# One hardware ring in planned order, the second channel matmul as seven products, and an earlier third batch: a change to a cosFormer-plus-mixer kernel

## The chip, the cores and the metric

The kernel runs on one core of a Trainium2 chip. The time is the device time of one execution in microseconds (us); lower is better. The profile comes from one execution; its span runs from the first to the last instruction.

## What is computed

Eight batches go through linear attention with cosine weights and then through a mixer layer, first over tokens, then over channels. From the reference, cut to what matters:

```python
B, H, S, D = q.shape                      # 8, 8, 576, 64
theta = np.pi / 2.0 * pos / S
def phi(x, c, s):
    r = np.maximum(x, 0.0)
    return np.concatenate([r * c, r * s], axis=-1)
q_p, k_p = phi(q, cos, sin), phi(k, cos, sin)
kv = np.einsum('bhsf,bhsd->bhfd', k_p, v)
z = np.sum(k_p, axis=2)
x = np.einsum('bhsf,bhfd->bhsd', q_p, kv) / (np.einsum('bhsf,bhf->bhs', q_p, z)[..., None] + 1e-06)
# x to (batch, 576, 512)
u = x + (np.maximum(x.T @ w_tok1, 0.0) @ w_tok2).T      # w_tok1 576x256, w_tok2 256x576
out = u + np.maximum(u @ w_ch1, 0.0) @ w_ch2            # w_ch1 512x1536, w_ch2 1536x512
```

## The kernel before, in words

A batch has 576 tokens. Two partitions share nine tokens: the even partition has the first four and the odd one the last four as token tiles 0 to 3, and the ninth is half of a fifth tile (j = 4, the tail). The tails of two batches are put together, so that channel work is done in nine groups of 4 x 128 tokens: groups 0 to 7 are the batches without their tails, group 8 holds all the tails (`group`, L277).

The attention of a batch runs over the five tiles j. `load` (L110) brings k, q and v as float32 into two sets of buffers (`raw`, b % 2), two DMAs each. `kfeat` and `qfeat` (L129, L134) make relu(x cos) and relu(x sin) of each tile in bfloat16: the cos half on VectorE (DVE, line L127), the sin half on ScalarE (ACT, L125). `vcast` (L145) casts v on GpSimd (POOL). `kv` (L165) multiplies features by v, with a column of ones for the sum z, in 40 matmuls of 65 columns; `kv_out` copies the result to SBUF on ACT. `qturn_dma` (L148) transposes a tile of q features by a DMA from SyncE's (SP's) queue. `num` (L186) multiplies them by kv, 8 matmuls a tile, and `x_out` (L194) adds 1e-6 to the denominator, inverts and multiplies on DVE.

The token mixer is `b1` (L206, 10 matmuls of 512 columns), `b1_out` (relu, ACT), `u_mm` (L224, two times four matmuls), `u_out` (L233, DVE: x is added, u is float32), `u_cast` (L237, ACT, to bfloat16) and `uturn_dma` (L244, two DMA transposes). For odd batches `tail_mm` and `tail_out` (L259, L270) do the tails of two batches.

The channel mixer of a group is `mlp1` (L282): 12 slots of four matmuls of 512 columns, each evicted with relu into `h1T` by `mlp1_out` (two of three on ACT, one on DVE); and `mlp2` (L296): four token tiles of 12 matmuls of 512 columns, in three parts each. `mlp2_out` (L301) adds u on DVE into a separate tile `res`, and ACT's queue stores it.

The order of work on each engine is written by hand. The head (up to about 24 us) does batch 0 in two halves of four heads. Then comes a stage with group 0's channel work, batch 1's attention and the loading and casting of the channel weights (L606 to L667). From there each group g has 24 slots, 12 of mlp1 and 12 parts of mlp2, and `plan_of(g)` (L718) puts the attention of later batches behind them: num, b1 and u of batch g + 1, and features, transposes and kv of batch g + 2. Group 1 is dense: it also has the features and kv of batch 2, and the plan loads batches 3 and 4 in it.

Transfers go over three queues: SP issues the first loads, the weights and all DMA transposes; ACT issues two weight loads and the stores; POOL issues the loads of batches 2 to 7. `load_late` (L709) lets POOL wait for a given eviction by a one-column copy before it issues loads.

Of the kernel before, what the change touches and what calls it, by code (L numbers as in the profile page):

```python
# [14 lines left out]
DEP = mybir.DependencyInfo(mybir.DependencyClass.Sync, mybir.DependencyReason.DATA)  # L15
# [3 lines left out]
def kernel(  # L19
# [14 lines left out]
    F = 2 * D  # L34
# [11 lines left out]

    NJ = 5  # L50
    T = 4

    const = ctx.enter_context(tc.tile_pool(name="const", bufs=1))

# [3 lines left out]

    ident = sb("ident", [P, P], BF16)
    cos_t = sb("cos_t", [P, NJ], F32)  # L60
    sin_t = sb("sin_t", [P, NJ], F32)
# [4 lines left out]
    wc2 = sb("w_ch2", [P, NCH, Dm], BF16)  # L66

    raw = {n: [sb(f"{n}_raw{i}", [P, H, NJ, D], F32) for i in range(2)] for n in "qkv"}
    kp = [sb(f"kp{j}", [P, H, 2, D], BF16) for j in range(NJ)]
    qp = [sb(f"qp{j}", [P, H, 2, D], BF16) for j in range(NJ)]  # L70
# [15 lines left out]
    res_all = sb("res", [P, 2, 2, Dm], F32)  # L86
    res = [res_all[:, i] for i in range(2)]
# [12 lines left out]


    def slots(b):

        return (0, 4) if b % 2 == 0 else (1, 0)

    def place(b, j):
        first, tail = slots(b)
        return tail if j == T else first + j

    def load(b, src, name, engs, h0=0, h1=None):  # L110
        h1 = H if h1 is None else h1
        dst = raw[name][b % 2]
        s = src[b].rearrange("h (i n) d -> i h n d", n=9)
        if b % 2 == 0:
            parts = ((1, 5, 9, 0), (0, 0, 5, 0))
        else:
            parts = ((0, 0, 4, 1), (1, 4, 9, 0))
        for (par, lo, hi, at), eng in zip(parts, engs):
            eng.dma_start(out=dst[par:P:2, h0:h1, at:at + hi - lo, :], in_=s[:, h0:h1, lo:hi, :])


    def feat(eng, out_ap, in_ap, tab, j):
        s = tab[:, j:j + 1]
        if eng is nc.scalar:
            eng.activation(out_ap, in_ap, AF.Relu, bias=0.0, scale=s)  # L125
        else:
            eng.tensor_scalar(out_ap, in_ap, scalar1=s, scalar2=0.0, op0=ALU.mult, op1=ALU.max)  # L127

    def kfeat(b, j, e0, e1, h0=0, h1=H):  # L129
        src = raw["k"][b % 2][:, h0:h1, place(b, j), :]  # L130
        feat(e0, kp[j][:, h0:h1, 0, :], src, cos_t, j)
        feat(e1, kp[j][:, h0:h1, 1, :], src, sin_t, j)

    def qfeat(b, j, e0, e1, h0=0, h1=H):  # L134
        src = raw["q"][b % 2][:, h0:h1, place(b, j), :]
        feat(e0, qp[j][:, h0:h1, 0, :], src, cos_t, j)
        feat(e1, qp[j][:, h0:h1, 1, :], src, sin_t, j)
# [6 lines left out]

    def vcast(b, j, eng, h0=0, h1=H):  # L145
        copy(eng, vb[j][:, h0:h1, 0:D], raw["v"][b % 2][:, h0:h1, place(b, j), :])

    def qturn_dma(b, j):  # L148
        nc.sync.dma_start_transpose(out=qpT[:, :, j, :],  # L149
                                    in_=qp[j].rearrange("p h a d -> p (h a d)"))  # L150

    def qturn_mm(j):
        ps = nextA()
        t = ps[:, 0, :].bitcast(BF16).rearrange("p (h t) -> p h t", h=H)
        for h in range(H):
            nc.tensor.transpose(t[:, h, :], qp[j][:, h, :, :].rearrange("p a d -> p (a d)"), ident)
        return t
# [3 lines left out]

# [3 lines left out]
    def kv(b, j):  # L165
# [3 lines left out]
        for h in range(H):  # L169
            nc.tensor.matmul(ps[:, h // HH, (h % HH) * E1:(h % HH + 1) * E1],  # L170
                             kp[j][:, h, :, :].rearrange("p a d -> p (a d)"), vb[j][:, h, 0:E1],
# [3 lines left out]
    def kv_out(b, eng):  # L175
        ps = kv_ps.pop(b)
        src = ps[:, :, 0:HH * E1].rearrange("p g (h e) -> p g h e", h=HH)
        dst = kv_sb[:, :, 0:E1].rearrange("p (g h) e -> p g h e", g=2)
        if eng is nc.scalar:
            eng.copy(dst, src)  # L180
        else:
            eng.tensor_copy(dst, src)
# [10 lines left out]

    def x_out(b, j):  # L194
# [3 lines left out]
        nc.vector.tensor_scalar_add(r, n[:, :, :, D], 1e-6)  # L198
        nc.vector.reciprocal(r, r)
        dst = x_sb[:, j, :] if j < T else x_tl[b % 2]  # L200
        rb = bass.AP(tensor=r.tensor, offset=r.offset, ap=[r.ap[0], [HH, 2], [1, HH], [0, D]])
        nc.vector.tensor_mul(dst.rearrange("p (g h d) -> p g h d", g=2, h=HH), n[:, :, :, 0:D], rb)  # L202
# [12 lines left out]
    def b1_out(b, mi, eng):  # L215
        ps = b1_ps[b]
        if eng is nc.scalar:
            eng.activation(B1[b % 2][:, mi, :], ps[:, mi, :], AF.Relu)  # L218
        else:
            eng.tensor_relu(B1[b % 2][:, mi, :], ps[:, mi, :])  # L220
# [4 lines left out]

# [7 lines left out]
    def u_out(b, c):  # L233
        ps = u_ps.pop((b, c))
        nc.vector.tensor_add(u_sb[b % 2][:, 2 * c:2 * c + 2, :], ps, x_sb[:, 2 * c:2 * c + 2, :])  # L235

    def u_cast(b, c, eng):  # L237
        dst, src = u_bf[:, 2 * c:2 * c + 2, :], u_sb[b % 2][:, 2 * c:2 * c + 2, :]
        if eng is nc.scalar:
            eng.copy(dst, src)  # L240
        else:
            eng.tensor_copy(dst, src)
# [17 lines left out]

# [9 lines left out]
    def tail_out(b):  # L270
        ps = u_ps.pop((b, "t"))
        nc.vector.tensor_add(u_tl[:, b // 2, :], ps[:, 0, :], x_tc)
        nc.scalar.copy(u_bt, u_tl[:, b // 2, :])
        nc.sync.dma_start_transpose(out=uTt[:, b // 2, :, :], in_=u_bt)

# [14 lines left out]
    def mlp1_out(mi, ps, eng):  # L290
        if eng is nc.scalar:
            eng.activation(h1T[:, mi, :], ps, AF.Relu)  # L292
        else:
            eng.tensor_relu(h1T[:, mi, :], ps)  # L294
# [6 lines left out]
    def mlp2_out(g, t, ps, last):  # L301
        r = res[(t // 2) % 2]
        nc.vector.tensor_add(r[:, t % 2, :], ps, group(g)[1][:, t, :])  # L303
        if g < B:
            if t % 2 == 1:
                o = out[g].rearrange("(i n) d -> i n d", n=9)
                j = t - 1
                nc.scalar.dma_start(out=o[:, j:j + 2, :], in_=r[0:P:2, :, :])
                nc.scalar.dma_start(out=o[:, 5 + j:5 + j + 2, :], in_=r[1:P:2, :, :])
        else:  # L310
            for par in range(2):
                o = out[2 * t + par].rearrange("(i n) d -> i n d", n=9)
                eng = nc.sync if par else nc.scalar
                eng.dma_start(out=o[:, 4, :], in_=r[par:P:2, t % 2, :])
# [9 lines left out]
    def bank_kv(hf):  # L324
        return psK[hf]

    def turn_half(hf, js, bank):
        t = bank.bitcast(BF16).rearrange("p (j h t) -> p j h t", j=2, h=HH)
        for i, j in enumerate(js):
            for h in range(HH):  # L330
                nc.tensor.transpose(t[:, i, h, :], qp[j][:, HH * hf + h, :, :].rearrange("p a d -> p (a d)"),
                                    ident)
# [6 lines left out]
    def kv_half(hf, j):  # L339
        ps = bank_kv(hf)  # L340
        for h in range(HH):
            nc.tensor.matmul(ps[:, h * E1:(h + 1) * E1],
                             kp[j][:, HH * hf + h, :, :].rearrange("p a d -> p (a d)"),
                             vb[j][:, HH * hf + h, 0:E1],
# [3 lines left out]
    def kv_half_out(hf, eng):  # L348
        src = bank_kv(hf)[:, 0:HH * E1].rearrange("p (h e) -> p h e", h=HH)
# [9 lines left out]
    def x_half(hf, js, ps, b, stages=(0, 1, 2)):  # L359
# [4 lines left out]
        if 0 in stages:  # L364
            nc.vector.tensor_scalar_add(rm, n[:, :, :, D], 1e-6)
        if 1 in stages:
            nc.vector.reciprocal(rm, rm)
# [5 lines left out]
        else:  # L373
            dst = x_tl[b % 2][:, c0:c0 + HH * D].rearrange("p (g h d) -> p g h d", g=1, h=HH)
        rb = bass.AP(tensor=r.tensor, offset=r.offset, ap=[r.ap[0], [HH, m], [1, HH], [0, D]])
        nc.vector.tensor_mul(dst, n[:, :, :, 0:D], rb)

    def b1_half(hf, js, bank, b):
# [432 lines left out]
```

## Time and profile before

| | |
|---|---|
| time, median of three runs | 305.77 us (305.6 to 306.41) |
| span of the profiled execution | 301.2 us |
| mean granted TensorE clock | 0.968 |
| TensorE matmuls (PE) busy | 261.9 us (87%), 1789 recorded |
| VectorE (DVE) / ScalarE (ACT) / GpSimd (POOL) busy | 156.6 / 131.0 / 75.3 us |
| DMA | 57.13 MB, 190 GB/s over the span |
| share of the chain that ended last | PE 67%, DMA 16%, DVE 8%, ACT 4% |
| first mlp1 matmul of groups 0, 1, 2, 3, 4 | 24.1, 61.9, 113.0, 143.5, 172.0 us |

The profile gives only the span of its own execution; it is 4.6 us below the median time.

How to read it: PE busy is the time in which a matmul was under way. Matmuls are pipelined, so the mean length of one (379 ns for 512 columns) is longer than the distance between two. "PEld" is the weight load. "PEclk" gives the granted TensorE clock in tenths of full speed, in 40 slices of the span of 7.5 us each. "DMA" is the mean busy share of the 16 DMA engines. In a table of groups the columns are line, engine, operation, output and inputs, shape, count, then busy us and mean ns of one, then idle time of the engine before them and what ended it. In the chain of waits, a piece is start, length, and what it was; the chain is followed backwards from the last instruction, so the pieces are what the end depended on. In a line on DMA issues the last number is the median time from issue to landing.

### The profile page before, as it was taken

How to read it: one execution, taken by the hardware profiler on the slowest of the kernel's cores; microseconds unless marked ns; L12 is line 12 of the kernel's file. 1: busy time of each engine (PE TensorE's matmuls, PEld its weight loads, DVE VectorE, ACT ScalarE, POOL GpSimd, SP SyncE). 2: the span in 40 equal slices, each digit the busy share in tenths (PEclk: the TensorE clock that was granted, in tenths of full speed). 3: DMA queues.
4: the chain of work that ended last, by engine and by line, in shares of the span. 5: the costliest groups of instructions: out<-in, count | busy, mean ns of one | idle time of the engine just before them, and what ended most of it. 6: DMA issues, size and time to landing. Idle time of an engine off the chain costs nothing.

```text
span 301.2 us, 4824 instructions
## 1 busy us (share of the span) xinstructions
PE 261.9 (87%) x1789; PEld 130.2 (43%) x1814; DVE 156.6 (52%) x341; ACT 131.0 (43%) x214; POOL 75.3 (25%) x134
## 2 busy tenths in 40 slices
PE   6789978977689009999989989999999999999993
PEld 2474455433235004545534544455455444444441
DVE  5965577494585002973566376828564552222221
ACT  5753744349544002474357346624753350410500
POOL 4399084370305000920710056040000100000000
PEclk9999999999999756999999999999999999999998
DMA  7999979579958980779993999493079114102012
GB/s 224 372 395 370 324 264 297 175 246 379 178 76 175 298 308 0 254 253 177 233 369 107 204 286 318 100 222 86 2 168 178 40 36 122 70 0 116 25 52 87
DMA packets 65655, 57.13 MB, mean 190 GB/s; under 512 B 48225, under 2 KB 55521, under 8 KB 65633
## 3 DMA queue, kind: packets, MB, share of 16 engines
q1 hardware_dynamic: 55968, 24.06, 34.3%
q0 software_dynamic: 5184, 21.24, 21.0%
q10 hardware_dynamic: 4480, 11.54, 10.9%
q8 instruction: 14, 0.23, 0.3%
q14 instruction: 9, 0.07, 0.1%
HBM read 35.85 MB, written 9.44 MB: 150 GB/s over the span
## 4 chain that ended last, share of the span: by engine, by line
PE 67%; DMA 16%; DVE 8%; ACT 4%; issue 2%; SPq 2%; DVEq 0%; ACTq 0%
PE psM L298 27%; PE psM L286 23%; DMA qpT<-qp 8%; DMA uT<-u_bf 6%; PE psA L212 5%; PE psA L230 5%; PE psA L170 2%; DVE qp L127 2%; DMA k_raw<-in_k_dram 2%; PE psA L190 2%; SPq L149 1%; DVE kp L127 1%; DVE res L303 1%; PE psA L266 1%; ACT kp L125 1%
## 5 line engine op out<-in xcount | busy, mean ns | idle before, releaser
L286 PE MATMUL psM<-uT,w_ch 128*128 128x512 bf16 x384 | 94.2, 387 | 18.6 <-DMA uT<-u_bf 14.8
L298 PE MATMUL psM<-w_ch,h1T 128*128 128x512 bf16 x414 | 100.1, 379 | 1.0
L292 ACT ACTIVATE h1T<-psM 128x512 bf16<-128x512 f32 x72 | 42.0, 595 | 83.3 <-PE psM L286 79.7
L286 PEld LDWEIGHTS <-w_ch 128*128 128x128 bf16 x432 | 40.5, 99 | 64.5 <-DMA uT<-u_bf 15.3
L298 PEld LDWEIGHTS <-h1T 128*128 128x128 bf16 x432 | 39.9, 98 | 43.6 <-issue 1.0
L303 DVE TENSOR_TENSOR res<-psM,u_sb 128x512 f32<-128x512 f32 x32 | 21.8, 689 | 38.4 <-PE psM L298 38.3
L294 DVE TENSOR_SCALAR h1T<-psM 128x512 bf16<-128x512 f32 x36 | 24.7, 686 | 23.9 <-PE psM L286 18.5
L143 POOL CAST vb<-v_raw 128x512 bf16<-128x512 f32 (+1 forms) x43 | 25.9, 638 | 44.2 <-DMA v_raw<-in_v_dram 32.9
L125 ACT ACTIVATE kp<-k_raw,sin_t 128x512 bf16<-128x512 f32 (+1 forms) x45 | 29.1, 668 | 5.5 <-DVE kp L127 4.2
L235 DVE TENSOR_TENSOR u_sb<-psA,x_sb 128x1024 f32<-128x1024 f32 x16 | 19.5, 1221 | 19.8 <-PE psA L230 19.6
L125 ACT ACTIVATE qp<-q_raw,sin_t 128x512 bf16<-128x512 f32 (+1 forms) x39 | 25.1, 683 | 7.7 <-DVE qp L127 7.6
L127 DVE TENSOR_SCALAR kp<-k_raw,cos_t 128x512 bf16<-128x512 f32 (+1 forms) x45 | 22.2, 526 | 1.9 <-DMA k_raw<-in_k_dram 1.9
L198 DVE TENSOR_SCALAR rden<-psA 128x8 f32<-128x8 f32 x35 | 5.6, 159 | 32.5 <-PE psA L190 32.0
L240 ACT CAST u_bf<-u_sb 128x1024 bf16<-128x1024 f32 x14 | 14.7, 1047 | 13.5 <-issue 6.7
L127 DVE TENSOR_SCALAR qp<-q_raw,cos_t 128x512 bf16<-128x512 f32 (+1 forms) x45 | 19.8, 469 | 0.8 <-DMA q_raw<-in_q_dram 0.8
L202 DVE TENSOR_TENSOR x_sb<-psA,rden 128x512 bf16<-128x512 f32 x28 | 19.4, 691 | 1.0
L190 PEld LDWEIGHTS <-qpT 128*128 128x128 bf16 x280 | 12.6, 98 | 16.0 <-DMA qpT<-qp 8.6
L190 PE MATMUL psA<-kv_sb,qpT 128*128 128x65 bf16 x280 | 14.2, 194 | 5.6 <-DMA qpT<-qp 4.5
L230 PE MATMUL psA<-B,w_tok 128*128 128x512 bf16 x64 | 16.4, 379 | 0.3 <-DVE B L220 0.3
L170 PEld LDWEIGHTS <-kp 128*128 128x128 bf16 x280 | 12.6, 98 | 8.9 <-DVE qpT L143 1.8
L218 ACT ACTIVATE B<-psA 128x512 bf16<-128x512 f32 x13 | 7.8, 598 | 19.9 <-PE psA L212 19.7
L170 PE MATMUL psA<-vb,kp 128*128 128x65 bf16 x280 | 13.6, 193 | 1.3 <-DVE qpT L143 1.3
(100 smaller groups left out, 193.9 us busy)
## 6 DMA issues: line engine op xcount, KB each, us to landing
out_dram<-res ACTq DMA_DIRECT2D x32, 256.0 KB, 4.1
k_raw<-in_k_dram POOLq DMA_DIRECT2D x6, 640.0 KB, 6.8
q_raw<-in_q_dram POOLq DMA_DIRECT2D x6, 640.0 KB, 10.5
v_raw<-in_v_dram POOLq DMA_DIRECT2D x6, 640.0 KB, 12.5
k_raw<-in_k_dram POOLq DMA_DIRECT2D x6, 512.0 KB, 5.6
q_raw<-in_q_dram POOLq DMA_DIRECT2D x6, 512.0 KB, 8.2
v_raw<-in_v_dram POOLq DMA_DIRECT2D x6, 512.0 KB, 11.4
res<-in_moe_w_ch_dram SPq DMA_DIRECT2D x2, 512.0 KB, 6.4
```

The lines of the kernel that those rows point to most:

```text
L125: eng.activation(out_ap, in_ap, AF.Relu, bias=0.0, scale=s)
L127: eng.tensor_scalar(out_ap, in_ap, scalar1=s, scalar2=0.0, op0=ALU.mult, op1=ALU.max)
L143: eng.tensor_copy(out_ap, in_ap)
L170: nc.tensor.matmul(ps[:, h // HH, (h % HH) * E1:(h % HH + 1) * E1], kp[j][:, h, :, :].rearrange("p a d -> p (a d)"), vb[j][:, h, 0:E1], st ...
L190: nc.tensor.matmul(ps[:, h // HH, (h % HH) * E1:(h % HH + 1) * E1], qpT[:, h, j, :], kv_sb[:, h, 0:E1], start=True, stop=True, skip_group_ ...
L230: nc.tensor.matmul(ps[:, half, :], w2[:, ki, 2 * c + half, :], B1[b % 2][:, ki, :], start=(ki == 0), stop=(ki == NT - 1))
L235: nc.vector.tensor_add(u_sb[b % 2][:, 2 * c:2 * c + 2, :], ps, x_sb[:, 2 * c:2 * c + 2, :])
L286: nc.tensor.matmul(ps.rearrange("p (t k) -> p t k", k=P), wc1[:, ki, mi * P:(mi + 1) * P], src[:, :, ki, :], start=(ki == 0), stop=(ki == ...
L292: eng.activation(h1T[:, mi, :], ps, AF.Relu)
L294: eng.tensor_relu(h1T[:, mi, :], ps)
L298: nc.tensor.matmul(ps, h1T[:, ki, t * P:(t + 1) * P], wc2[:, ki, :], start=(ki == 0), stop=(ki == NCH - 1))
L303: nc.vector.tensor_add(r[:, t % 2, :], ps, group(g)[1][:, t, :])
```

## The change

1. Second channel matmul. Groups 1 to 8 no longer use `mlp2`. The product h w_ch2 is cut into 2 x 2 blocks over (token half i, hidden half kh) and (hidden half kh, column half c), and made from seven block products in place of eight, each of 12 matmuls with 256 columns. Four sums of blocks of w_ch2 are made once on DVE (`w_sums`). Four sums of blocks of h1 are made in each group (`h_sum`): 0, 2 and 3 on DVE, 1 on POOL. The products go to three PSUM banks; products 4, 5, 3 and 2 are accumulated onto banks that were already read once. Six adds on DVE (`add_to`) and three on POOL (`add_p1`, after ACT has copied the first product) sum them into `u_sb` itself, and the stores read `u_sb`. The tile `res` is gone. Group 0 still uses `mlp2`.
2. Features. They are r = relu(x) and r tan(theta). The cosine goes into v (and into the column for z), and the query's cosine cancels in the quotient, so that 1e-6 becomes 1e-6 / cos. The r half of all five tiles is one instruction (`rfeat`: DVE in the head, POOL later), the r tan half is one per tile (`tfeat`, on ACT, some on DVE early). `vcast` is a multiplication by cos.
3. Transfers. All loads, DMA transposes and stores of the groups are issued by SP, in the order of the plan (the first loads and the last group's stores still use ACT too). k, q and v have one buffer each, with six places, in place of two buffers.
4. Plan. Each step has a position (a number), and the steps are issued in the order of the positions. Batch 2's features and kv are in group 0's stage and its num, b1 and u at the start of group 1; kv of batch 3 is in group 1, and so on. num of the first two tiles of batch g + 2 stands at the end of group g. Batch 1's u is transposed by DMA and no longer by TensorE. The u casts move from ACT to POOL.

The core of the diff (old functions that are only taken away are left out):

```diff
-    raw = {n: [sb(f"{n}_raw{i}", [P, H, NJ, D], F32) for i in range(2)] for n in "qkv"}
+    wt = sb("w_ch2t", [P, 4, NQ, HC], BF16)
+    raw = {n: sb(f"{n}_raw", [P, H, NJ + 1, D], F32) for n in "qkv"}
-    res_all = sb("res", [P, 2, 2, Dm], F32)
+    hs = sb("h1s", [P, 4, NQ, 2 * P], BF16)
+    p1 = sb("p1", [P, 2, HC], F32)
...
+    def rfeat(n, b, eng, s0=0, s1=NJ, h0=0, h1=H):
+        at = first_place(b)
+        src = raw[n][:, h0:h1, at + s0:at + s1, :].rearrange("p h j d -> p j h d")
+        relu(eng, feats[n][:, s0:s1, h0:h1, 0, :], src)
+    def tfeat(n, b, j, eng, h0=0, h1=H):
...
+        s = tan_t[:, j:j + 1]
+        if eng is nc.scalar:
+            eng.activation(dst, src, AF.Relu, bias=0.0, scale=s)
+        else:
+            eng.tensor_scalar(dst, src, scalar1=s, scalar2=0.0, op0=ALU.mult, op1=ALU.max)
...
-        nc.vector.tensor_scalar_add(r, n[:, :, :, D], 1e-6)
+        V.tensor_scalar_add(r, n[:, :, :, D], eps_t[:, j:j + 1])
...
+    def w_sums(n, eng):
+        a, b_, o, op = ((wq(0, 1), wq(0, 0), wt[:, 0], ALU.subtract), (wq(1, 1), wq(0, 1), wt[:, 2], ALU.subtract),
+                        (wq(1, 1), wt[:, 0], wt[:, 1], ALU.subtract), (wq(1, 0), wt[:, 1], wt[:, 3], ALU.subtract))[n]
+        eng.tensor_tensor(out=o, in0=a, in1=b_, op=op)
+    def h_sum(n, eng, k0=0, k1=NQ):
+        a, b_, o, op = ((hq(0, 0), hq(1, 0), hs[:, 2], ALU.subtract), (hq(1, 0), hq(1, 1), hs[:, 0], ALU.add),
+                        (hq(1, 1), hs[:, 2], hs[:, 1], ALU.subtract), (hq(0, 1), hs[:, 1], hs[:, 3], ALU.subtract))[n]
+        eng.tensor_tensor(out=o[:, k0:k1], in0=a[:, k0:k1], in1=b_[:, k0:k1], op=op)
+    def product(n, bank, first, ts=(0, 1)):
+        lhs, rhs = prods[n][0](), prods[n][1]()
+        for ki in range(NQ):
+            for t in ts:
+                nc.tensor.matmul(bank[:, t * HC:(t + 1) * HC], lhs[:, ki, t * P:(t + 1) * P], rhs[:, ki, :],
+                                 start=(first and ki == 0 and t == 0), stop=(ki == NQ - 1 and t == 1),
+                                 skip_group_check=True)
+    def add_to(g, i, c, bank, ts=slice(0, 2)):
+        u = uq(g, i, c)[:, ts, :]
+        V.tensor_add(u, bank2(bank)[:, ts, :], u)
+    def add_p1(g, i, c, eng):
+        u = uq(g, i, c)
+        eng.tensor_add(u, u, p1)
...
+    order2 = (1, 7, 6, 4, 5, 2, 3)
+    for g in range(1, B + 1):
+        b, f = g + 1, g + 2
+        for s in range(NCH):
+            at(s, m1, g, s)
+            at(s + 0.6, m1_out, s, V if s in (0, 4, 7, 9) else A)
+        for i, n in enumerate(order2):
...
+                at(NCH + i, prod_step, g, n)
...
+        at(6.3, h_sum, 0, V)
+        for p in range(3):
+            k0, k1 = 2 * p, 2 * p + 2
+            at(7.9 + 2 * p - 0.2 * (p == 2), h_sum, 2, V, k0, k1)
+            at(8.8 + 1.5 * p, h_sum, 1, G, k0, k1)
+        at(12.6, h_sum, 3, V)
+        at(12.9, lambda: A.copy(p1, bank2(bank[1])))
+        at(12.91, add_p1, g, 0, 1, G)
+        at(13.9, quarter, g, 1, 1, 7)
+        at(13.91, add_p1, g, 1, 1, G)
...
+        if g < B:
+            at(16.95, store, g, 1, (SY, SY))
+            at(18.9, quarter, g, 0, 1, 6)
+            at(18.95, store, g, 0, (SY, SY))
...
+            pn = [0.2, 1.2, 2.2, 3.2, 4.2] if g == 1 else [None] * 2 + [0.2, 1.4, 2.6]
+            pb, pu, pt = (5.6, 7.8, None) if g == 1 else (4.9, 6.9, 8.9)
...
+            for c in range(2):
+                at(pu + c, u_mm, b, c)
+                at(pu + c + 0.1, u_out, b, c)
+                at(pu + c + 0.2, u_cast, b, c, G)
+                at(pu + c + 0.25, uturn_dma, b, c)
...
+            for j in range(NJ):
+                at(tk[j], tfeat, "k", f, j, A)
+                at(tq_[j], tfeat, "q", f, j, A)
+                at(tq_[j] + 0.05, qturn_dma, f, j)
+                at(pv[j], vcast, f, j, G)
+                at(pk + 0.1 * j, kv, f, j)
+            at(pk + 0.6, kv_out, f, A)
+            for j in range(2):
+                at(pnn[j], num, f, j)
+                at(pnn[j] + 0.1, x_out, f, j)
+            if f + 1 < B:
+                at(18.0, rfeat, "k", f + 1, G)
+                for n, p in pl:
+                    at(p, load, f + 1, n, (SY, SY))
+        run_all()
```

The positions not shown: r features of q at 3.0 and k's tan features from 1.2, q's from 8.5; v casts from 5 to 10; kv at 13.2; num of the next batch at 17.0 and 18.2; loads of k at 8.3, of q at 12.5, of v at 13.0.

## The prediction

> **What bounds the kernel now.** I read the page's slices first, then the chain of waits in order of time, then the table by stretches, then the groups by shape and the DMA issues. The slices:
>
> ```profile
> PE   6789978977689009999989989999999999999993
> PEclk9999999999999756999999999999999999999998
> DMA  7999979579958980779993999493079114102012
> ```
>
> TensorE (PE) is full except in the first three slices, a thin stretch in slices 5 to 12 and one hole in slices 14 and 15, with the granted clock at 5 and 6 tenths around it. The chain names the hole:
>
> ```profile
> 95.31 17.67 DMA uT<-u_bf
> 112.98 0.05 issue
> 113.03 3.17 PE psM L286 x7
> ```
>
> The last matmul before it ended at 98.2, so PE stood 14.8 us until the transposes of u (L245) landed. After it, the whole chain shows 12 matmuls in 5.30 us where the group runs at 0.215 each (4 in 0.86): 2.7 us more at the halved clock. Why the transposes were late, by stretches (length, busy us of PE, PEld, DVE, ACT, POOL, then PEclk, DMA share, GB/s):
>
> ```profile
> 74.00:82.00 8.00, 5.52 (x53) 2.42 (x53) 3.74 (x10) 4.96 (x10) 2.85 (x5) 1.00 1.12 201
> 99.00:111.00 12.00, 0.00 (x0) 0.00 (x0) 0.00 (x0) 0.00 (x0) 0.00 (x0) 0.59 1.04 339
> 152.00:158.00 6.00, 5.95 (x35) 2.82 (x37) 3.25 (x9) 2.69 (x6) 0.00 (x0) 1.00 1.02 356
> 143.50:172.00 28.50, 27.14 (x193) 13.55 (x195) 16.40 (x35) 14.62 (x24) 7.14 (x12) 1.00 0.88 233
> ```
>
> In 99:111 no engine works, and the DMA is full at 339 GB/s: the loads of batch 4, issued on POOL's queue from 93.98, fill it, while two transposes from SP's queue get a small part. Alone (74:82, eight of them due) transposes move 201 GB/s. The last row is a period of the steady part, the one that starts at 143.53 and ends when the next group's first matmul starts, 171.95: 28.4 us, 27.2 of it PE work and 1.2 waiting for qpT. So: PE work bounds nearly everything, the loads' collision with the transposes costs 17.5 us once, and the rest is a second stage (24.1 to 61.9) with about 6 us of short waits.
>
> **The parts, in us of the span (301.2; the median of the runs is 305.8, 4.6 above it, and I add those 4.6 at the end).** The rows I use:
>
> ```profile
> L298 PE MATMUL psM<-w_ch,h1T 128*128 128x512 bf16 x414 | 100.1, 379 | 1.0
> L235 DVE TENSOR_TENSOR u_sb<-psA,x_sb 128x1024 f32<-128x1024 f32 x16 | 19.5, 1221 | 19.8 <-PE psA L230 19.6
> L681 POOL TENSOR_TENSOR x_tc<-x_tl,x_tl 128x512 bf16<-128x512 bf16 x3 | 3.8, 1264 | 40.9 <-DVE x_tl L202 40.9
> L143 POOL CAST w_ch<-u_tl 128x512 bf16<-128x512 f32 x4 | 2.3, 615 | 0.0
> qpT<-qp SPq DMA_TRANSPOSE x30, 3.8
> uT<-u_bf SPq DMA_TRANSPOSE x12, 2.7
> ```
>
> *Seven products.* A mean of 379 ns is a matmul's latency; they follow each other every 0.215 us (4 in 0.86). Per group the second channel matmul is 48 of them: 10.3. Afterwards it is 7 x 12 = 84 of 256 columns. The b1 halves of the head (L383) have that form: 10 in 1.09, each with its own weight load, so 84 x 0.109 = 9.2. Saved: 1.15 a group, 9.2 over groups 1 to 8. Group 0 keeps the old form.
>
> *The sums for the products* lie beside PE. DVE per period: h_sum 0, 2, 3 are 3 x 1536 bf16 elements from SBUF. No row shows this form: at best 0.67 ns an element (DVE's copies of 1024 bf16 take 0.685), at worst 1.35 (the 512-element multiply, 691 ns): 3.1 to 6.2, and I take 4.5. Five or six quarter adds (0.69 each) replace four result adds. With 4 of 12 h1T evictions, x_out and u_out, DVE stands at some 17 to 20 of 26: not the bound. POOL gets three h_sums and three adds of p1 (six at the 1.26 of L681: 7.6), u casts (2 x 1.0), five v casts (5 x 0.6), two r features of 2560 elements each (2 x 2.4 when 512 take 0.6 and the fixed part is about 0.15), 0.9 for the tail: 18 of 26. A POOL form that is half or double that speed bounds it at 13 and 28. POOL loses six load issues (about 0.69 each). ACT loses the u casts (2 x 1.05) and gains the copy of p1 (0.6); its eight evictions and ten features stay.
>
> *One ring.* The 17.5 go: a transpose can no longer share the engines with a load that was issued after it. What is late next is whatever stands ahead of it in the ring. Work of one period there: seven transposes of 256 KB at 1.3 (201 GB/s) to 1.6 (144 GB/s at share 0.90 in 86:92), say 1.5: 10.5, and 0.75 for the tail's in most periods; three loads, 3.54 MB at 356 (on POOL's queue) to 369 GB/s (26:34, on the ring of SP): 9.7; stores, 1.05 MB at some 400: 2.6. Sum 22.8, 23.5 with the tail.
>
> *A new wait.* The result is now summed into u_sb itself and stored from there, so u_out of batch g+1 (DVE, line 248 of the new kernel) waits for the stores of batch g-1 to land; they are last in the ring of the period before. Behind u_out on DVE stand the eviction of slot 7 and the next half sums; behind its result POOL's cast and the u transposes, the first in the ring of the next round. So the ring is a loop: 22.8 to 23.5 of transfers, then landing of the store (some 1.3: the 2.1 of a 128 KB store less its issue and transfer), u_out 1.22, cast 1.0, issue 1.0 (a transpose takes 1.23 on SP): 4.5. One round: 27.3 to 28.0, against 26.0 to 26.9 of PE work (27.2 less 1.15, and 0.86 for the tail product in odd batches). Nearly equal; the ring is the longer.
>
> *Batch 2's attention earlier.* kv(2) (40 matmuls, 1.25) moves into stage 0, and batch 1's u is transposed by DMA, not by 16 PE transposes (0.9). Stage 0 holds 32.2 of PE work. Its end waits: u_mm, u_out 1.22, cast 1.05, issue and landing some 4, behind three parts of mlp2 and kv(2) (3.8): 3 open. Before, this corner cost 1.4, but three waits for features and q transposes on PE, at 38 to 46, cost 1.1, 1.3 and 0.7. I price 4 of waits against 5.9.
>
> *Features r and r tan.* Head: one relu over five slots (DVE, about 0.75) for five that start 0.26 apart; of 8 features a half on ACT 6 stay. Only the head is chain-bound by them: -0.5 (0 to -1.5). The cos goes into v's cast, the same count. raw has one buffer, so batch 1's load waits for batch 0's features (done by 15 in this trace) and casts (16); the ring is busy with weights till about 25 anyway: 0.
>
> **The sum.** Group 1 starts at 24.1 - 0.5 + 32.2 + 4 = 60 (now 61.9). From there the ring: in it stand k of batch 3, three q transposes, q, v, stores: 3.2 + 4.5 + 6.5 + 1.3, so u_out(2) can start at +14, its transposes at +18. Four rounds with loads, 27.7 each: +129. After the last u transposes start, the period's remainder (slot 11, seven products, kv, two num, less what ran already) is 11: group 6 starts at 60 + 140 = 200 (now about 228). Group 6: 10.3 + 9.2 + 5.5 = 25; groups 7 and 8 are 19.5 each; 1.5 of waits: 65.5. End after the last matmul 4.3 (now 4.6, the last store is half as big). Span 269.8, time **274**.
>
> **A rule that speaks against it.** DVE's rows show POOL in its way: its features of q take 0.48 each alone and about 0.83 while POOL casts v (39.4 to 41.7). The Trainium skill (SBUF — State Buffer, section Who interferes with whom) says that a DVE instruction with two SBUF inputs and a GpSimd one that reads SBUF exclude each other, and the second waits for the whole of the first. The trace before has no such DVE instruction of size. By the rule the five half sums a period on DVE each wait for up to one POOL operation, the long relu included: as an estimate 3 more a period, 284 in all. My sum takes only what the features show.
>
> **Rivals.**
> - *The ring is not the bound* (PE is): if transposes run at 1.3 and the turn takes 3.5, a round is 25.5. Groups 1 to 5 then take 132.8 of PE work and some 3 of waits: span 265.4, time 270 and down to 264 with no waits.
> - *POOL and DVE block each other*: POOL at 18 busy plus waits for loads (r of q, v casts) and for DVE; u's cast and the half sums come late, 2 to 3 a period over groups 1 to 5: 279 to 290, centre 284. For it: the 0.83. Against: both have 7 us free in a period.
> - *Slower*: the ring drains at every change of kind (transposes, k, transposes, q and v, stores), each costing a landing. From 1.6 a change up, with four new changes in each of five rounds, that adds 32 and the kernel is above 306. For it: no queue here mixes the two kinds, SP's held transposes alone in the steady part. Against: in 224:232 stores and transposes of two queues run side by side at 215 GB/s and a DMA share of 1.33. At 2.0: 314.
> - *The products don't pay*: if 256 columns cost the weight load too (98 ns beside 109), nothing is saved: +9, 283. The L383 row speaks against it.
>
> **Chances.** Ring-bound 274 (270 to 279): 0.45. PE-bound (264 to 270): 0.23. POOL and DVE (279 to 290), with the products not paying: 0.22. Slower: 0.07. Below 264: 0.03. Range 264 to 288, which leaves out the last two and the end of the third. About 0.3%, 0.9 us, is what this kernel's measurement can tell from no change; within it lies 0.01, slower 0.07, faster 0.92.
>
> **What would show it.** No gap over 3 us on PE after 62 and no half clock. Products at 0.109 each. In periods of groups 2 to 5 a length of 27 to 28, u_out waiting for DMA of out, and a DMA share of 0.85 or more; if instead PE waits less than 1 a period, the PE case holds. POOL under 20 a period; its r features at about 2.4. Wrong if loads and transposes in one ring are slower than apart, or if DVE's half sums are far above 1.6.

## The result and the profile after

The changed kernel takes **325.77 us** (median; 324.8 to 326.28), against 306.09 for the kernel before beside it (median of four, one of them 312.89): ratio 1.063, 95% interval 1.058 to 1.068. I had forecast 274, faster. The profiled execution has a span of 323.0 us, 21.8 longer than before, at a mean granted clock of 0.912 (before 0.968).

These are the slices of the changed kernel, 8.1 us each; PE, PEclk and DMA answer to those shown of before, POOL is new.

```profile
PE   6789749966797599779985997979958999999993
POOL 4599999994999997999899879999997128346081
PEclk9699978995998599799997899899995999999998
DMA  6999968149962989189938991599565305301103
```

The hole of before is gone, as forecast: PE has no slice at 0. The half clock that I had ruled out has not gone: several slices show a granted clock of 5 to 8 tenths. In place of the hole PE is thin in every period up to slice 31, and POOL is at 9 almost without a break to that same slice. POOL was busy for 75.3 us before; it is now for 258.6. A period of the middle (length, then busy us of PE, PEld, DVE, ACT, POOL, clock, DMA share, GB/s):

```profile
185.90:219.80 33.90, 29.04 (x239) 18.05 (x236) 22.80 (x34) 12.76 (x22) 32.27 (x18) 0.95 0.74 190
```

POOL works for 32.3 of 33.9 us. The ring, which I had made the bound, is at a share of 0.74. POOL's groups by shape (busy us, mean ns of one) say what fills it:

```profile
L160 POOL TENSOR_SCALAR vb<-v_raw,cos_t 128x512 bf16<-128x512 f32 x33 | 58.0, 1763 | 0.0
L134 POOL TENSOR_SCALAR qp<-q_raw 128x2560 bf16<-128x2560 f32 x7 | 46.8, 6679 | 2.5 <-DMA q_raw<-in_q_dram 1.4 <-issue 1.1
L134 POOL TENSOR_SCALAR kp<-k_raw 128x2560 bf16<-128x2560 f32 x7 | 46.7, 6674 | 4.4 <-DMA k_raw<-in_k_dram 4.4
L321 POOL TENSOR_TENSOR h1s<-h1T 128x512 bf16<-128x512 bf16 x24 | 29.6, 1245 | 20.2 <-DVE h1T L134 19.7 <-ACT h1T L132 0.6
L128 POOL CAST u_bf<-u_sb 128x1024 bf16<-128x1024 f32 x12 | 12.4, 1036 | 5.8 <-issue 4.3 <-DVE u_sb L248 1.5
```

The last two cost what I took. The first three don't: a relu of 2560 elements takes 6.68 us where I took 2.4, a multiplication by the cosine 1.76 where I took 0.6. Both are TENSOR_SCALAR, 2.6 to 3.4 ns an element; my row was a CAST, 1.2. How this reaches PE is in the chain of waits (start, length, what):

```profile
199.72 1.14 POOL vb L160
...
201.24 1.04 POOL u_bf L128
202.28 1.71 POOL vb L160
203.99 0.95 POOL u_bf L128
204.95 1.81 POOL vb L160
206.76 1.12 POOL h1s L321
207.89 0.75 POOL u_bt L128
208.63 3.79 POOL vb L160 x2
212.43 0.04 issue
212.47 0.41 PE psA L188 x8
```

For 12.7 us the end of the kernel hangs on POOL's queue alone: v casts, u casts and a half sum, one behind the other, until kv (L188) can run on PE. PE waits 21.5 us in all for vb in 16 places. A little later the same chain reads:

```profile
214.79 1.28 SPq L169
...
216.17 2.45 SPq L169
...
218.68 0.63 SPq L122
...
219.36 5.88 DMA q_raw<-in_q_dram
...
225.50 3.03 POOL qp L134
```

In SP's queue the load of the next batch's q (L122) stands behind transposes of this batch's q features (L169), and POOL's next long relu of q waits for that load (0.5 us; its relu of k fills the time before), with the next v casts behind it. So two bounds lie close together in this period: POOL's summed work, and a loop over POOL's operations and transfers that are issued in one order.

The granted clock is a part of the loss too. The share that was not granted comes to 28 us of this span (0.088 of 323.0), against 10 before (0.032 of 301.2). That is an estimate from the two means, and how much of it PE would have used is not shown.

### The profile page after: what moved, and what is told of

Read it like the earlier page. It is cut to its first block, busy times and chain, and to the rows that moved or that the text cites. A ratio compares the mean times of both kernels' runs of the same rounds, so it can differ in the third digit from the quotient of the medians.

```text
span 323.0 us, 5456 instructions
## 1 busy us (share of the span) xinstructions
PE 272.1 (84%) x2086; PEld 168.9 (52%) x2086; DVE 208.1 (64%) x328; ACT 114.6 (35%) x195; POOL 258.6 (80%) x172
## 3 DMA queue, kind: packets, MB, share of 16 engines
q10 hardware_dynamic: 1024, 1.05, 1.0%
## 4 chain that ended last, share of the span: by engine, by line
PE 39%; POOL 17%; DMA 16%; issue 8%; DVE 7%; SPq 7%; ACT 4%; ACTq 0%; POOLq 0%; DVEq 0%
PE psM L295 15%; PE psM L332 14%; POOL vb L160 10%; DMA k_raw<-in_k_dram 8%; DMA q_raw<-in_q_dram 5%; SPq L169 4%; POOL qp L134 4%; DVE kp L152 2%; POOL u_bf L128 2%; DMA out_dram<-u_sb 2%; PE psA L230 2%; SPq L122 2%; PE psM L372 2%; DMA h1T<-in_moe_w_tok_dram 2%; DVE w_ch2t L315 1%
## 5 line engine op out<-in xcount | busy, mean ns | idle before, releaser
L160 POOL TENSOR_SCALAR vb<-v_raw,cos_t 128x512 bf16<-128x512 f32 (+1 forms) x41 | 65.3, 1601 | 4.9 <-DMA v_raw<-in_v_dram 4.9
L344 DVE TENSOR_TENSOR u_sb<-psM,u_sb 128x512 f32<-128x512 f32 x42 | 28.8, 686 | 44.8 <-PE psM L332 43.0
L134 POOL TENSOR_SCALAR kp<-k_raw 128x2560 bf16<-128x2560 f32 x7 | 46.7, 6674 | 4.4 <-DMA k_raw<-in_k_dram 4.4
L134 POOL TENSOR_SCALAR qp<-q_raw 128x2560 bf16<-128x2560 f32 x7 | 46.8, 6679 | 2.5 <-DMA q_raw<-in_q_dram 1.4
L321 POOL TENSOR_TENSOR h1s<-h1T 128x512 bf16<-128x512 bf16 x24 | 29.6, 1245 | 20.2 <-DVE h1T L134 19.7
L332 PEld LDWEIGHTS <-h1s 128*128 128x128 bf16 x384 | 38.8, 103 | 9.8 <-issue 3.8
L332 PE MATMUL psM<-w_ch2t,h1s 128*128 128x256 bf16 x288 | 39.2, 293 | 2.6 <-DVE h1T L134 2.6
L188 PE MATMUL psA<-vb,kp 128*128 128x65 bf16 x280 | 14.7, 210 | 22.7 <-POOL vb L160 21.5
L321 DVE TENSOR_TENSOR h1s<-h1T,h1s 128x512 bf16<-128x512 bf16 (+1 forms) x32 | 27.8, 875 | 7.3 <-ACT h1T L132 5.5
L348 POOL TENSOR_TENSOR u_sb<-u_sb,p 128x512 f32<-128x512 f32 x21 | 26.9, 1303 | 4.7 <-DVE u_sb L344 4.7
L150 ACT ACTIVATE kp<-k_raw,tan_t 128x512 bf16<-128x512 f32 (+1 forms) x38 | 25.4, 685 | 5.3 <-DMA k_raw<-in_k_dram 5.3
L188 PEld LDWEIGHTS <-kp 128*128 128x128 bf16 x280 | 12.6, 108 | 25.2 <-issue 22.5
```

Of the source, the lines that this page charges most:

```text
L134: eng.tensor_relu(out_ap, in_ap)
L150: eng.activation(dst, src, AF.Relu, bias=0.0, scale=s)
L160: eng.tensor_scalar_mul(dst, src, s)
L321: eng.tensor_tensor(out=o[:, k0:k1], in0=a[:, k0:k1], in1=b_[:, k0:k1], op=op)
L332: nc.tensor.matmul(bank[:, t * HC:(t + 1) * HC], lhs[:, ki, t * P:(t + 1) * P], rhs[:, ki, :], start=(first and ki == 0 and t == 0), stop= ...
L344: V.tensor_add(u, bank2(bank)[:, ts, :], u)
```

## The experiments

Theory at the start: **POOL's form** (the tensor-scalar operations cost 2.8 to 2.9 times what I took, and POOL bounds the period). Rivals: the lock between POOL and DVE that I had named; the ring and u_out's new wait for the stores; products that don't pay. The runs fall on several chips, on which the kernel before took 305.6 to 308.6 in the median; so a difference between kernels of different chips (e5 and e1, say) can be off by some 3 us.

### POOL's form, or the lock

**e1**: the same places, but plain copies on POOL (relu and cosine are left out there).

```diff
-        relu(eng, feats[n][:, s0:s1, h0:h1, 0, :], src)
+        (copy if eng is G else relu)(eng, feats[n][:, s0:s1, h0:h1, 0, :], src)
-            eng.tensor_scalar_mul(dst, src, s)
+            (eng.tensor_copy(dst, src) if eng is G else eng.tensor_scalar_mul(dst, src, s))
```

> On POOL, the r features are plain casts (no relu) and the v casts lose their factor cos: the same elements in the cast form. This part of the computation is left out. Theory (the form: POOL's tensor-scalar operations cost 2.6 to 3 ns an element and make POOL the bound): the r features fall from 6.67 us to about 2.6, the v casts from 1.6 to 0.6, POOL's work in a period from 32.8 to about 19, and the time from 326 to 275 to 290. Rival ring (the order of transfers on one queue and u_out's wait for the stores bound a period at 30 or more): POOL gets faster, but the time stays above 300. Rival products (the seven products cost more than they save): above 300 too, with PE full.

Measured 295.71, ratio 0.971 (0.963 to 0.979). That is above the theory's 275 to 290 and below the 300 of both rivals, and 30 us less than the changed kernel. The copies cost what I had taken for the relu:

```profile
L128 POOL CAST qp<-q_raw 128x2560 bf16<-128x2560 f32 x7 | 16.3, 2334 | 22.6 <-DMA q_raw<-in_q_dram 21.5 <-DVE h1T L134 1.0
L160 POOL CAST vb<-v_raw 128x512 bf16<-128x512 f32 x33 | 26.7, 827 | 7.6 <-DMA v_raw<-in_v_dram 7.6
```

POOL goes from 258.6 to 163.5 us busy. So the price of the form is worth 30 of the 52 us between forecast and result; the other 22 are elsewhere. By the starts of the groups in the two traces, e1's span of 293.7 is 1.9 shorter in the head, 12.4 in group 0's stage, 8.1 in group 1 and only 6.7 in groups 2 to 5. There a round falls from 33.8 to 32.2 us in the mean, and something else holds it.

**e2**: each long relu on POOL in five pieces of 512.

```diff
+        for p0, p1_ in (((i, i + 1) for i in range(s0, s1)) if eng is G else ((s0, s1),)):
+            src = raw[n][:, h0:h1, at + p0:at + p1_, :].rearrange("p h j d -> p j h d")
+            relu(eng, feats[n][:, p0:p1_, h0:h1, 0, :], src)
```

> Each r feature on POOL as five operations of 512 elements in place of one of 2560; all else as in the changed kernel. Theory of the form: POOL's work stays at 33 us a period or grows a little, the time is 322 to 335. Rival lock (the damage is done by single long POOL operations that keep DVE out, not by POOL's load): DVE's operations no longer stretch to 3 to 6 us, and the time falls to 295 to 310.

Measured 324.21, ratio 1.065 (1.059 to 1.071): no change. Yet the lock is real. In the changed kernel a VectorE feature that starts in the shadow of a POOL relu ends only after it (timeline: start, length, engine, line):

```profile
36.76 6.81 POOL L134 TENSOR_SCALAR qp<-q_raw 128x2560 bf16<-128x2560 f32 x1
...
37.58 7.09 DVE L152 TENSOR_SCALAR kp<-k_raw,tan_t 128x512 bf16<-128x512 f32 x2
```

and the half sum of 1536 elements on DVE takes 3.08 us in the mean there. In e2, where the means of POOL's forms are 1.6 us at most, it takes 0.96. First the changed kernel, then e2:

```profile
L321 DVE TENSOR_TENSOR h1s<-h1T 128x1536 bf16<-128x1536 bf16 x8 | 24.7, 3084 | 14.7 <-ACT h1T L132 14.7
```

```profile
L322 DVE TENSOR_TENSOR h1s<-h1T 128x1536 bf16<-128x1536 bf16 x8 | 7.7, 963 | 14.7 <-ACT h1T L132 14.7
```

These 17 us of DVE time go (32.6 with its other operations: 208.1 to 175.5), and the span stays (323.0, 323.6): the blocked time was not what PE waited for. POOL's work grew a little, to 265.8 us. The long blocking of the half sum is what the Trainium skill (SBUF — State Buffer, section Who interferes with whom) describes for a VectorE operation with two SBUF inputs beside a GpSimd one that reads SBUF. The rule holds here in its direction; its price for this kernel, as it stands, is nil. (The feature in the first view has one tensor input, so that sentence of the page is not about it.)

**e3, e4**: move the work off POOL. e3 puts the r features on DVE (`rfeat(..., G)` becomes `V`, at positions 3.5 and 6.0); e4 also puts the v casts on ACT (in the head on DVE and ACT in turn).

> The r features go from POOL to DVE (2560 elements, about 1.8 us by the 0.94 of its 1280 in the head), with their positions a little later; the v casts stay on POOL. Theory of the form: POOL's work falls by 13.3 us to about 19.5 a period, PE is the bound again or nearly: 283 to 298. Rival ring: above 300. Rival lock: about the same as the theory of the form.

> As the kernel with r on DVE, and the v casts on ACT (0.6 each), in the head on DVE and ACT: POOL has no tensor-scalar operation of size left, some 11 us a period. Theory of the form: 270 to 285, and the head ends at 24 again and not at 26.8. Rival ring: a period of groups 2 to 4 stays at 28 or more with u_out waiting for the stores, 285 to 300.

Measured 320.4 (ratio 1.051, 1.044 to 1.057) and 308.19 (1.011, 1.004 to 1.018). Both missed my expectation by over 20 us, though POOL is busy for only 52% and 35% of the span; e3 lies where its ring rival had it (above 300), e4 above its rival's range as well (285 to 300). In groups 2 to 5 of e3 POOL works 74.5 us in place of 125.0, and the four rounds take 136.5 us in place of 135.4. Two things in the traces: in e3 the v casts on POOL (1.71 each) still stand in the chain just ahead of kv, behind a load of v that POOL waits 64 us for in all; and a relu of 2560 elements on DVE takes 2.81 us (I had taken 1.8) and stands in order ahead of x_out. This is e4's chain at the start of a period:

```profile
178.64 2.81 DVE kp L134
181.45 0.14 DVE rden L216
...
181.85 0.70 DVE x_sb L219
182.55 0.04 issue
182.59 0.60 PE psA L205 x8
```

So an engine's total is not enough: what stands in its queue ahead of a piece that PE waits for counts in full. In the steady rounds "POOL's sum is the bound" is not the explanation, or not the only one. In group 0's stage it fits: there POOL is busy for 49.3 of 50.0 us in the changed kernel, and in e2 the chain of that stage runs from 50.7 to 78 us through POOL's operations alone.

### The new wait

**e5**: e1 with three buffers for `u_sb` (`u_sb[b % 3]`), so that u_out of batch g + 1 waits for the stores of g - 2.

> As e1 (POOL's r features and v casts are plain copies, so relu and the cosine are left out there), and u_sb has three buffers, so u_out of batch g+1 waits for the stores of group g-2, not g-1. e1 took 295.7; its chain holds 25 us of waiting for stores of u before u_out. Theory of the new wait (the loop over u's buffer and the ring bounds a round of 31 us): the loop is cut, u_out comes when its matmuls are done, rounds go to PE's 27 to 28, 278 to 287. Rival, the ring itself is full (its throughput bounds a round): the wait only moves to the transposes or to the loads, 291 to 297.

Measured 282.59, ratio 0.915 (0.908 to 0.923), in the theory's range: 13 less than e1, all of it in groups 2 to 5 (13.9 by the traces). This is the wait that the prediction named; e1's chain shows it (a store, then u_out), with rounds of 31 us from one such u_out to the next:

```profile
136.16 0.38 SPq L362
136.59 8.46 DMA out_dram<-u_sb
145.13 1.23 DVE u_sb L248
```

The rest of the round is not the one that I had described. From one such store (136.2) to the next (167.1) the chain has the store with 9.0 us, u_out and other DVE work 3.9, POOL's u and v casts and a half sum 4.9, kv and products on PE 7.6, and x_out with result adds on DVE 5.6. None of the ring's transposes and loads is in it, of which my round was made. I had taken 1.3 us for the landing of a store beyond its issue and its transfer; its median from issue to landing is 7.4 us in the changed kernel, and 2.5 where the loads are in another queue (e10 below), so most of it is queueing behind the loads. The ring's throughput itself is not the bound: with the loop cut it carries the same 56 MB in 281 us.

### The products

**e6**: e1 with the old second channel matmul in groups 1 to 8. **e11**: the changed kernel with that alone undone.

```diff
-        for i, n in enumerate(order2):
-            if g < B or n != 3:
-                at(NCH + i, prod_step, g, n)
...
+        for t in range(4):
+            for part in range(3):
+                at(NCH + (3 * t + part) * 7 / 12, m2, g, t, part)
+            at(NCH + (3 * t + 3) * 7 / 12, m2_out, g, t)
```

> As e1 (relu and cosine left out on POOL), but groups 1 to 8 use the old second channel matmul (12 matmuls of 512 columns for each token tile), with no half sums, no weight sums and no adds of the first product; only the result adds on DVE stay. If the products are worth 1.15 a group wherever PE is the bound and the ring bounds groups 1 to 5: three to four groups pay, 299 to 301; if PE bounds all: 304 to 306. Rival, the sums on DVE and POOL cost more than the products save: 285 to 294.

> The changed kernel with one part alone undone: groups 1 to 8 use the second channel matmul of 512 columns, without half sums, weight sums and adds of the first product. The whole result is computed. POOL loses six two-input operations of 1.27 a period (7.6 of its 33 to 37). If POOL's summed work is the bound of a round, rounds 1 to 5 shorten by 5 to 7 each, PE's work in groups 6 to 8 grows by 3.5: 295 to 305. Rival (not the sum but the places of the long operations hold PE up): 312 to 326.

e6: 287.63, ratio 0.932 (0.924 to 0.940), 8 less than e1: by the traces 11.6 shorter in groups 2 to 5 and 3.0 longer from group 6 on. e11: 318.94, ratio 1.046 (1.039 to 1.053), 7 less than the changed kernel, where I had expected 20 to 30. In both the products cost more than they save, which was the rival in e6's expectation. That e11 moved so little, with POOL at 192.1 us (61%), is what its rival had: the places of the long operations, not POOL's sum, hold PE. Its chain, like the changed kernel's, runs in turn through loads of k and q (12.6% and 11.8% of it from 120 to 215 us) and POOL's relus and casts.

**e13, e14, e15**: on the best kernel without products (e9 below), products in groups 6 to 8 only, in groups 1 to 5 only, and not at all, on one chip.

> As e9, with the seven products (and all that goes with them) in groups 6 to 8 only; the weight sums are made in groups 4 and 5. The whole result is computed. These groups have little or no attention beside them. If the products pay 1.15 in a group whose DVE and POOL are free: 3 to 4 faster than e9, 280 to 282. Rival (the chain of sums holds the products up even there): 284 to 288.

> As e9, with the seven products in groups 1 to 5 only. The whole result is computed. e8 (products in all eight) took 298.6 and e9 (none) 284.6, so the two parts must add up to +14. If the loss is made where attention work fills DVE and POOL: 16 to 19 over e9, 300 to 304. Rival (the loss is spread over all groups): 8 to 10 over e9, 292 to 295.

> e9 once more, as the measure beside the two others on the same chip: 283 to 286 by either theory.

Measured 283.04 (ratio 0.926, 0.921 to 0.930), 305.17 (0.993, 0.986 to 1.001) and 285.51 (0.934, 0.929 to 0.938). The early groups lose 20 us in the medians (14 between the two profiled executions, of which e14's is the shortest of its four and e15's the longest of its six). The late ones gain 2.5, between the theory's 3 to 4 and the rival; the two intervals just overlap. The chain of e13 shows the gain where it was priced, 9.17 for 84 products against 10.36 for 48 matmuls of 512 columns (here those of mlp1, of the form and number of the old second matmul), and groups 6 and 7 take 25.0 and 19.5 us in e13, 26.2 and 20.7 in e15:

```profile
229.22 9.17 PE psM L328 x84
238.39 10.36 PE psM L291 x48
248.75 9.17 PE psM L328 x84
```

In e14 (1 us above the theory's range) the chain runs through DVE just before the products of group 2:

```profile
121.98 1.17 DVE h1s L317
123.15 2.25 DVE qp L142 x3
125.40 1.30 DVE h1s L317
126.73 1.79 DVE h1s L317
128.52 0.61 DVE u_sb L340
129.17 4.09 PE psM L328 x36
```

Three half sums, three features of q and a result add stand in a row for 7.1 us, and PE's next products wait for the end of it. In groups 6 and 7, with no features beside them, the products run in one piece. That the loss comes with what DVE and POOL do beside the products fits e5 and e8 too: both have the products in all eight groups and differ in the features alone (plain copies on POOL in e5, the cosine form on DVE in e8), and they lie 16 us apart (282.59 and 298.56). A kernel like e5 without the products was not run.

### The features part, the ring, and what is left

**e7**: the changed kernel with features by cos (DVE) and sin (ACT) per tile, v cast plainly on POOL, a column of ones. **e8**: with three `u_sb` as well. **e9**: with the old second matmul as well. **e12**: e9's plan with the new features kept, r and v casts on DVE, r of q on ACT. 

```diff
-        relu(eng, feats[n][:, s0:s1, h0:h1, 0, :], src)
+        eng.tensor_scalar(dst, src, scalar1=cos_t[:, j:j + 1], scalar2=0.0, op0=ALU.mult, op1=ALU.max)
-            eng.tensor_scalar_mul(dst, src, s)
+        copy(eng, vb[j][:, h0:h1, 0:D], src)
```

> The changed kernel with its features part undone: relu(x cos) per tile on DVE, relu(x sin) per tile on ACT (head too), v cast plainly on POOL, a column of ones, 1e-6. The whole result is computed. POOL loses the two long relus and the slow v casts (about 33 a period goes to some 13), DVE gains ten features of 0.48 a period (about 5). Theory (POOL's form is the main cause, DVE has room): 292 to 302. Rival (DVE becomes the bound, or its two-input sums are blocked whatever POOL does): 305 to 318.

> As e7, with three buffers for u_sb. The whole result is computed. If the wait of u_out for the stores is what is left after POOL's form: 10 to 17 faster than e7, 278 to 290, and faster than the kernel before. If the ring's throughput is: within 3 of e7.

> The changed kernel's ring and plan with both other parts undone (features by cos on DVE and sin on ACT, v cast plainly on POOL; second channel matmul of 512 columns in groups 1 to 8) and three buffers for u_sb. The whole result is computed. e8, with the products, took 298.6; e6 showed 8 less without them at a free DVE. Theory (ring and plan pay once nothing loads POOL and DVE): 276 to 288, faster than the kernel before by 18 to 30. Rival (DVE's features in order of the plan still hold PE up, or the ring bounds a round): 290 to 300.

> The features part kept (r, r tan, cosine in v), but off POOL: r of k and the v casts on DVE, r of q mostly on ACT; the second channel matmul of 512 columns; three buffers for u_sb. The whole result is computed; the head is the changed kernel's. If POOL's form was the features part's only fault: 275 to 285, within 4 of e9. Rival (a relu of 2560 elements is as harmful in DVE's or ACT's order, as e3 and e4 hint): 290 to 300.

e7: 305.86 (ratio 0.988, 0.976 to 0.999). That is above the theory's range and in the rival's (305 to 318): POOL is free (44%), but DVE, with ten features more a period, is busy for 218.6 us (e1: 187.7), and its half sums and q features are 13% of the chain, the landing of stores 11%. e8: 298.56 (0.968, 0.959 to 0.978), 7 less than e7 by the third buffer; I had expected 10 to 17, and 278 to 290 in all. e9: **284.55** (0.933, 0.928 to 0.938). Ring and plan alone, with the third buffer, are 7% faster than the kernel before, in the theory's range. A middle period of e9:

```profile
128.77:155.81 27.04, 27.04 (x196) 13.55 (x194) 17.85 (x36) 12.15 (x21) 5.58 (x7) 1.00 0.90 241
```

27.04 us long, of which PE works 27.04, at full clock, with the ring at a share of 0.90: this is the period that the prediction wanted. Two of the four rounds of groups 2 to 5 are like this; the others take 28.6 and 29.5. e12: 298.20 (0.978, 0.973 to 0.984), 14 slower than e9 where I had allowed 4: the rival's range. Its head is the changed kernel's and starts the channel work at 27.3 (e9: 24.2); in groups 2 to 5 the 2.81-us relus on DVE stand in the chain ahead of x_out as in e4, beside loads of v and transposes of q. So off POOL the new features still cost, and one long instruction for five tiles makes the first tile as late as the last. How much of the 14 is due to that no run separates; on POOL, five pieces in place of one gained nothing (e2).

**e10**: e9 with the loads of batches 2 to 7 on POOL's queue at the same positions (`load(..., (SY, SY))` becomes `(G, G)`).

> As e9, but the loads of batches 2 to 7 are issued at the same positions on POOL's queue, so that only the one-ring part is undone. The whole result is computed. Theory (a load beside a transpose starves it, as in the hole of the kernel before): 8 to 18 slower than e9. Rival (the plan's places alone keep loads and transposes apart, or loads beside stores gain what transposes lose): within 3 of e9.

Measured 321.47 to 334.29 in four runs (median 328.21); the fastest is 37 above e9's median, and the profiled execution is the longest. Four times its chain waits 12.8 to 16.0 us for a transpose of q; this is the first of them, and then the same stretch by engines (columns as in the period above):

```profile
93.75 7.58 DMA k_raw<-in_k_dram
101.33 16.00 DMA qpT<-qp
...
117.38 0.62 PE psA L201 x8
118.00 1.71 PE psM L368 x4
```

```profile
101.00:117.00 16.00, 4.99 (x30) 2.02 (x27) 2.35 (x5) 0.72 (x1) 0.00 (x0) 0.73 1.12 194
```

A transpose of q takes 16 us to land beside loads of another queue, with the DMA engines at a share of 1.12 and PE at 5 of 16. The median transpose of q takes 5.9 us to land, against 3.4 in e9. This is the hole of the kernel before, period after period (44.4, 38.6, 38.1 and 36.1 us for groups 1 to 4, where e9 has 33.4, 29.5, 27.0 and 28.6); I had expected 8 to 18, too little, because I took it for a single collision. The stores, in a ring without loads, land in 2.5 us (median, 7.8 in e9). The Trainium skill (DMA: Bandwidth & Descriptors, section Queues, rings and completion order) says that an engine takes turns between its queues packet by packet; the trace agrees in that both streams move at once; how the turns fall between them it does not show.

## Why the prediction was wrong, point by point

- *What bounds now* (of the kernel before): right. The collision of loads and transposes is a cost of two queues: one ring removes it (no hole in the changed kernel), and e10 brings it back. With one ring, e9 reaches a period of PE work alone.
- *The sums for the products*: **this step failed.** Its terms for POOL, "two r features of 2560 elements each (2 x 2.4 ...)" and "five v casts (5 x 0.6)", were priced by the row of a cast. They measured 2 x 6.68 and 5 x 1.76. The sum of 18 becomes 32.3 of a 33.9-us period. I had written the bound for a POOL form of half or double the speed (13 and 28), and then neither carried the 28 to a rival nor looked for a row of the right form: the POOL two-input rows (2.5 ns an element) stood in the same list and were the nearer ones. e1 prices the step at 30 us. What the runs do not settle is its path in the steady rounds: the sum on POOL, or the places of the long relus and v casts in a loop with the loads (e3 and e11 speak for the places).
- *One ring and a new wait*: the wait of u_out for the stores was named and is there; e5 prices it at 13 us. The loop around it was not right. I had put 22.8 to 23.5 us of the ring's transfers in a round; e1's round of 31 us has only the store of them (9.0, of which I had sized 1.3 as landing), and the rest is POOL, PE and DVE work. In the changed kernel the ring was at a share of 0.74 and not the bound.
- *Seven products*: right in size (84 in 9.17), wrong in sign over the kernel. The term that was missing is the waiting for the sums: DVE "at some 17 to 20 of 26, not the bound" is a statement on a total, and the sums wait in DVE's order behind features (e14's chain). Groups 1 to 5 lose 20 (e14), groups 6 to 8 gain 2.5 (e13) of the 3.5 priced. My rival of products that don't pay had another reason (weight loads), which the 9.17 refutes.
- *Batch 2 earlier*: stage 0 takes 50.0 us (26.8 to 76.8), where I had 36.2. Its chain has VectorE's features under POOL's relu (7.09 for two) and the weight sums (4.79 for two, ahead of u_out). But e2, without the long relus, takes 51.9, and e1, with copies on POOL, 37.6: POOL's price makes nearly all of the difference, and 4 us of waits was then too little by 1.4 only. With the old features on DVE and ACT (e9) the stage takes 41.5.
- *Features r and r tan*: the head is 2.7 longer, not 0.5 shorter. Three v casts of 0.92 on POOL stand in its chain; with copies in their place (e1) it is 0.8 longer.
- *The sum*: by stretches, the head gives 3.2, stage 0 13.8 and the five rounds of groups 1 to 5 36.7 of the 53.2 us between the two spans (the parts are rounded in the prediction's sum); from group 6 on, 69.5 against 69.8, it was right; POOL has no features left there.
- *The rule against, and the rivals*: "POOL and DVE block each other" named the right two engines, but by the lock, at 284. The lock is there (17 us of half sums on DVE go in e2) and costs no time here. The slower rival, a ring that drains at each change of kind, is refuted by e9: the same mixed ring at a share of 0.90. The result lies above all that I had priced (314 was the highest). The rival that was missing is POOL at the price of its true form.

Still open: how the loss of the products in groups 1 to 5 divides between DVE's order, POOL's order and the transfers that move with them, and why the third buffer is worth 13 after e1 but 7 after e7. No run separates these.

## What to carry to other kernels

Price an operation by a row of its own form on its own engine; where there is none, take the nearest form that does arithmetic, not a cast, and if a bound so found makes an engine the longest of the period, it is a rival with a price, not a remark. Then ask of each moved piece what stands ahead of it in its engine's order and who waits for it: DVE at 56% of the span held PE up in e12. Here transposes and loads did best in one queue in planned order (e9 against e10), and what was stored through that queue needed one more buffer than the count of its users suggests (e5, e8). And when one cost is taken away, look for the next bound close behind it: in groups 2 to 5 e1 gained only 6.7 us, because u_out's wait came next.

## What the runs showed of the hardware

- POOL: a relu or a multiplication by a per-partition number, float32 to bfloat16, takes 2.6 ns an element at 2560 (the relu, 6.68 us) and 1.5 to 1.76 us at 512; a cast of 2560 takes 2.33, of 1024 1.04 and of 512 0.61 (weights) to 0.83 (v in e1). One relu of 2560 is 12% cheaper than five of 512 (1.51 each in e2).
- DVE: the same relu takes 2.81 us for 2560 elements, ACT 2.34. Its half sum of 1536 takes 0.96 in e2, where the means of POOL's forms are 1.6 us at most, and 3.08 in the mean beside POOL's long relus.
- In one ring (e9) and in two (e10), stores and transposes trade places: by the medians stores land in 7.8 us against 2.5, transposes of q in 3.4 against 5.9; the longest transpose of q takes 7.7 against 16.0.

The fastest version that computes the whole result is e13 (one ring, old features, three `u_sb`, products only in the last three groups): 283.04. The ranges of its runs and of e15's overlap (281.16 to 284.63, 283.86 to 287.09).
